# Linear tables by wide products, a shorter way to the mean of h, two more idle products and another written order

## The chip, the core and the metric

The kernel runs on one core of a Trainium2 chip. Its engines work side by side, each through its own queue in order: PE (TensorE) multiplies matrices and writes to PSUM, ACT (ScalarE) and DVE (VectorE) read PSUM and SBUF, POOL (GpSimd) reads and writes SBUF and starts some of the transfers, SP (SyncE) starts the others. The metric is the device time of one execution in microseconds (us), the median of the runs shown.

## The reference

Two attention steps over four batches of 12416 rows with 128 channels, and then a feed-forward network on every row:

```python
def mab(q, kv):
    s = scale * (q @ kv.transpose(0, 2, 1))
    s = s - s.max(-1, keepdims=True)
    a = np.exp(s)
    a /= a.sum(-1, keepdims=True) + 1e-09
    return a @ kv
h = mab(I, x)          # 32 inducing rows, per batch
attn = mab(x, h)       # every row of x is a mean of the 32 rows of h
gate = np.maximum(attn @ w_gate, 0.0)          # 128 -> 1536
out = (gate * (attn @ w_val)) @ w_out          # 1536 -> 128
```

`x` is (4, 12416, 128), `inducing` (32, 128), the weights have 1536 hidden channels, and the output is (49664, 128) in float32.

## The kernel before

**What it computes instead.** A row of the attention output is a weighted mean of 32 vectors. Where a hidden channel's gate has one sign for all 32 of them, the network's output for a row is a quadratic form in the row's 32 weights. The kernel builds this form once per batch as tables, and checks at the end that the signs were as assumed (if not, a general kernel runs; it doesn't here). With p the 32 exponentials of a row, the output is a sum over squared differences (p_m - p_n)^2 times tables `T`, plus a sum over p_m^2 times a linear table `L`, divided by the square of the sum of p.

**Stages of one batch b (1 to 3).** POOL starts the loads of x as float16 chunks of 16 row tiles (`x16`, line 237). Each chunk is transposed to `xT`, by PE with copies on DVE or ACT (lines 780 to 787) or by a transposing DMA on SP's queue (line 769). PE multiplies with the inducing rows (line 796), ACT takes exponentials (801), PE sums (810, 815), DVE adds up in `hz`. `h_join` and `h_centre` divide and centre h, giving `hT`. Gate and value products follow (line 898), DVE and ACT bring them to SBUF as `ga` and `va`, products of the two (lines 950, 957, 988, 1002) are multiplied by `w_out` on PE into the tables (lines 963 and 1007). Batch 0 is done first, by `first_batch`, from loads through SP.

**The output stage.** Each chunk of 2048 rows (`Q`, 24 of them and one for the rest) goes through: scores (PE, line 511), exponentials `p` (ACT, 520), p squared (POOL or DVE, 530), differences (PE, 567: four groups of 32 rows side by side, two of them into the tile `dd`, two into other banks), squares of `dd` (ACT, 581), squares of the other two banks (ACT at 593, or DVE copies at 595 and POOL or DVE multiplies at 599), 64 output products with T (PE, 625) and 16 with L (614), the division by the squared sum (DVE, 655), and the store on SP (673, 676). The squared reciprocals come from lines 545 (DVE) and 550 (POOL or DVE).

**The order.** From the tables of batch 0 on, every step (1588 or so of them) stands in a text, `ORDER`, three or more letters a step: which step, which engine, which of the rotating buffers (six PSUM banks `mb`, twelve `F`, and so on), and whether PE does some idle products first. Engines execute their steps in the order of the text, each waiting for what it needs. A choice that a step leaves open (DVE or POOL, DVE or ACT; a PE sum of two tables by 24 products, "left apart", in place of an addition at line 1002 and 12 products; transposing by PE or DMA) is made in the text too. A second rule holds in `in_turn`: a POOL step of some kinds (products of `ga` and `va`, their sums, squares, zq) waits for the last DVE step of these kinds that stands before it.

**The places that the change touches.** `centre` takes h (32 columns in float32) and writes `hT`: h times 64 minus its mean, then h times 64 twice, then the mean. Before, DVE sums h (line 246), scales the sum (247) and then subtracts (250), scales twice (259) and copies (267). At the end of `first_batch`, `idle` has PE do three products that nobody reads (line 358), while DVE computes h. `lin(b, 2)` adds the two halves `lt` of the linear table's operand, 384 elements a partition, and `lin_mm` multiplies it by `w_out` (line 963): for each of 12 groups of hidden channels four products with the same 32 columns, into the four groups of 32 PSUM partitions, so that the table stands there four times over. It is needed four times since p squared lies in four groups of 32 partitions.

Of the kernel before, what the change touches and what calls it, by code (L numbers as in the profile page):

```python
# [9 lines left out]
FP32 = mybir.dt.float32  # L10
# [93 lines left out]
Lo0M60Oz00Le000050Ov04P103LU0N94Mp4LK4P302MG0O+2P02O-2011Ow2Oy2Ox2P21H609E0GE006001002e052P41022007  # L104
10u0310I9042B0812f10J1PD2PB2PE2PC20CC015A0A10K10G10E10D10v10M1PP0PQ00PJ0PK048M0PL0PM0PN01M0PR0PS0PG
2PI2PH2P62P520O00519PT0Pb0Pc030x020P10S10Q1PO2P720y2PF2Pd0Pe0Me00+00428Pf07U0LY0611020z3PV30w32LW05
M+00U003041210-1Pg2LZ2PU2042LX1Li072Lj21G003171H11I2FM0Lg001m040P805Lh2P921K1PA11A002361C21B11n11E1
Ls080Lt2PW01PX0Lq05NV01131D2Pa214002051511811620d04Ck00b010Z0Lr20f00a0MT00W01y003241c050Y01b01d01+2
0531731o311J30c201z1201MA090MB2M8030e0Ni00g01s001234s02E01P00LL40Ly4M921e03+01i0La0030h21w21f251t11
u11h00o041g028002120q0Lb10m050p01j02912C21k20X022003110k00r01S000l00j01Q02A12312612411-22g20LQ0121T  # L110
0MI010s240n2MJ2LR11O042q0053ALz430i41l40t43641p011q22u12s12r11R0LS02EU0Lc01MR3MS30LT21U231Y0Lk013A6
04O051Ll12w00209Ld2Ph21r22D22y22+24P12x11V0Lm01Lu0031X01W04Q22Md31Lv14U0052B3W0004V14Y13X1Ln21Z24W2
2z31x2Mo322J012L0Lw032k004502K02I0Lx22m22o22l1M2012MC0032Q00M312G02-32p24X3Mz33MD130004573112N0M402
2M213422P02O0MK013321ML13c00158M522R24R02ME04MM033d13g13e14S2MF2MN2Mg010MO22a02Mi04Mh2MP032H05Mj1MQ
23o00106N8343532n34T3NJ352Z02V02b02Y02W02h043q13s13p12U02T02c222i22X22j23Y31NU3Ps01Pm03Pq00Pt1Pr13u
00245Pn2Pp2Po2H+0Pi053G013N003Z033H03I03M0Pj2Pl2Pk23v13w13y13a23B053F03O03i0032137043j13k13m13A03L0
3T03S03D03Q03R0P-2P+2Pv33J203P25Pu24m001323b3Pw34J003C03U24o14q14n13E21a42S4NK45k4Mq423V4A+4O244E02
4G0N20544D04I04F04L04K0N316c04a00134410Q12Q02Q624e14c1Px0570042QC27114b1Pz14203Q701Q804H24Q23QD04QE
0QB2Py25G020QH24g001534M25H1MX0444h1MY24504404702NL47NA40OD42d44004k15S000474904304A07305480Q325U15
W146235I305T152005104z04680314i16917424B24u05e00520Q52QI25g14w0NX014-05J035004x0Dc04y053215f1NY24+2  # L120
5i1Q435705550580Mk0005605Y0012AMl15K24v0459255444N4MV03QJ00QK05C05D05B0MW26A21QO25Z15c15a15M00539QN
15Q15N15A0MZ012QP01QQ0Jk0N0005O25E25P3Ng372326E00358QT2Ma1N12Mm046201Mb026F16G26I1Nh31Mc26K00036640
6B055-026505z06006306L16O1Mn25L26M2QU26C26W004055l0356a16Y25r05v05+06X1Mv0006N36H366226125o05q0Mw16
74OZ44C46Q004116R18m0207u0015w05p06U26S27v18n15s215t0N40115u07C004035x27x03Nm062N516V36T37G15y45F4I
s4Nt4OO43K4Mx01Nk056r006t07D17E17y2Nn2Ns306Z38o30753My26D37I00322NF001N604Nl2N727K27L3O1327z36u06s0
NQ0157J1NG17M16f047O00134NR16v247P17S26y0NH026w06e050NI27Q1760032B7T2OC337w317717827A26m06x0NZ0016z
06n06l0Na19e0326+2792ON348A0012A9f16o0NS048B16p22Nb036g06h06i06j0NT2Nc2Nd28E18C17+00040Ne036k27m027
r017l07k0Ke07j0Ok0OY357B3Oj3Nf28017-18217X084005097n238518627p0Qd037o07q0Qe17s2Qf04QV028738G0053788
1Qg1QW2QY2QX2QZ018I18H18K1Qa2Qc2Qb27a007b07Z07g047Y07W08s00258Qn2Qo28u18w18t1Qi39g328e017f07e07d08c
08b08d0AW0317h217c28P02AX192005468f259418p008R038T08i08Y018W09316q46-4O343Nu48OE498O08q29619q000519  # L130
s1Qv2Qp2Qq28X08g08V09h048h0AZ008Q09r1Qh39i2Aa29u18Z208y004058S0Qw05Om018j0Q-2901Qx0R0008U28k28z1On1
Q+1R10Qj38r39800314Qt29C2R428+1Qk059918l4D8020D91Qm19A19a049Y0Qs29b0A000102Bs09H029W09Z0A21A11A41Qr
2Ql29D39c229U09K03No0119T09V0Np1Qu29I0Ao00543OP44Aq1R52Ap19J09N009O09L09P09Q09X2RB39G0As19w0015B9M2
49R29x1Oa45Nq02R604R70Nr29+29y1Ai00309Aj1O8002Nz0119-39j3DA31RA2Ak2Am2RC05N+1O91RD09k004307i49l1AH0
0AG0N-019o2RG2BO0229m1Ac0035AAn2O029p3AY30Al3BP1Ag2Ad1AD01OJ014BR02AI0AB0A80OK1BS2Ae2Bm00527Bn1Bo2A
F0AC0AA0OA03AJ25Bq1BU00458OB2AE2BV1Ah3Af3BT3Ab3Bp3OL009S48a49d47t4BY2OU003AT02Oo011AQ0OM2BW2OV1Op1A
u00505A903Ay2Aw2Av1CG041BZ3Ax3BX3Az3BQ32DB01AR0Oq00AS0AO0CH1DC2Of015CM00146Og1CO2CN1AL0AM0AN0OW05AU
21Oh01CQ1OX2AP2Oi2Or2Bg00254Bk1B204B50B40BG03BD0B30Bi2Bh1Os2A-010Ba00522B624Bb1BE0B70BF0BI0B90Bc2Bj
3DD3Bd3CI30BH20Be1CY00450B80BA0CZ1Ca2BB2BJ0BL0BK0Cc1CS00231C004By01CJ05BM2AV4AK4BC4BN4E0002CT1Bu0CW
2CK2CU2E11Ce0035BB-0Cf1Cg2E300Ot02C10Bw0Bx0E42Ou2Ci1DQ0030ADS1DR1Bz0C805C20C70C60C50CB03B+22C32Bv0D  # L140
U1CL3CV3E53CX3Cb3Ch3CP3E232DE00219C923RM04DI1DF1RI00RS05RN2RP2RQ01CD0CC0CA0RO2RT2RR1DG1RJ2RL2DK0045
5RK2CE2DL1RH2Rg2DO1DM1Cq01Cp0Co0Eu021Cr0E600033E71Cu05Cv0Cm0Ct0Cw0EA2RU3Cs21EB3DW00432Cx2Ev1E81DY1C
+01Fm020D00Cz0C-0D200DX1Rd2Rc2Cn0Fn1F400547D40D30D50Dg02Dh0Di0D125Ew30F51F82F61Da1Ra2Fy00144De05Dj0
Fz1D62RV3Dk24Do0Dl0Dn0Dm0EO00308Rb2F+1G01EP1Dp2Dy02Dx0Dz0Dt01Ds0Dw0Df0Ri2EQ1ES1EI00456Du0Dr0D+20Re3
EJ1Ro0Rp03Rj00Rk0Dv2D-4D74CF4C44Cy4EC00210Rq0EK1EM1EG2Rn2ED1Ex04Rr0Ge052Rs0Ey2Rf2EE1Gf1E+00101Rt2F0
2EH3E-1EY04Ed02Ef0Ea0Eg0EW0Rh2F21Gk0053BEe0Gl1RW3Eh20Eb0EZ0Ej01El0Ek0Ec2FA0002AGo1Gm1Ru2Em0FB1Eo03E
p0Er0Eq0FC2EX0FE1R+2Fs00455Rv00Ft1Rw0En25RX02Rz2Es2FG00102F93Gg31Ez3Fo32Fw1Fu1R-05RZ1FI2RY2S00FH1IO
031S32FO041FK2IP1G200259FJ2G31FQ0Fp00FR0FS0Fq2G42FX0FT0G61Ia00303FL3FU23Ib1Ic2FV0FY0FW0Fg02G53F13FD
3FP05Ie1FZ2G800430G91GC2GA2Fi0Fc0Fh0HW000HX1Gq00138GB2Fb0Gs2Gr1Fe0GI04GL0Fd0Gu1Fr2GD3Ff22Gw00016Gy2
Gx1HY30Id3Gz3Gt3GJ0GO03Fj0GK0Fk2GG0G+1Hu00507GM21Hw2Et4Fa4Ei4Hv1GQ0GN0GP0GT02GU0GW0GR2Hy1Hc00141Hd1  # L150
He2IR05Ga00Gb0Gh03GV0GH0IS2Gi2Hg1H00015AGX25H11H22HB03GZ0GY0HC0H804Gc2H41Gj3Hf3H33Ho00212Hp1Hq2Hs2I
Q32Ht3IT3Hx3HA0HH0HG0HD0L4002L51IU00520HE23IV1IY2HF0HS01HR0HI0H900IW1HJ2Hi00329Hj1Hm2HN0HZ05HL0HQ0H
a2HT0KA040Hk1HU20Im00254KB1Iq2Hb3Hr3Hn3In1HM0IE03IL01HO0IK0I10Io1HP2SA2KM00455HK4GS4KO2KN1II0IG0IJ0
ID0IF0KQ1KY00026KZ1I204I40I705I30Ir3KP3KC31IZ3I00IM23IH2Kc2Ka1Ig0013BIh1Ii2I90I50L702I80IA0L82I621J
G001Ik1KG00128IB2JH1J504Iw03Ix0J60KI2KK2Ij3KH1J80J105J70HV4IN4Dq4Fl4IC4KS0001AIt02KW1S42S72J920KJ3L
93JI30Kd3KT1J00I-0JB0J20JD0Iy0Iz0J323KU1Je00141I+2Jf1JA0Kk05JC0Kq00Ko0Ji2Kg0JE2Jg1JM00342Kl0KD02JN1
JO2KE2Kj0Kr0Ku01Ki0KF3JQ1JP3KL3JS00329Km24Kp0Kx0Kv0Kw0JT1Ks2JW2Kh04J44Gd4Kt4JF4JU1JY00507Jc1L10K+0J
J03L00J+02JZ1S92Ky22Kn4Kz4K600K-0JK2SB2JL2JX2Jn0Ja1L22LA00133Jj3L632K50K40K70J-0K10K00K821K22LC1LD1
LB1Jw05Ju0Jx0Jv0S52Jm01L34K94Jr0Jy23K34Jz4S604SC2S82Jp0Jo0Jq0LE03LF0Js2LG0LH0SD2Jt4LI25SE00SF2LJ4SG
4"""  # L160
# [7 lines left out]
def square_body(ctx, tc, x, inducing, moe_w_gate, moe_w_val, moe_w_out, out):  # L168
    nc = tc.nc
# [74 lines left out]
    def centre(b, h):  # L244
        hb = st([P, 2], FP32, "hb", 2)
        nc.vector.tensor_reduce(out=hb[:, 0:1], in_=h, axis=AX.X, op=ALU.add)
        nc.vector.tensor_scalar(
            out=hb[:, 1:2], in0=hb[:, 0:1], scalar1=HS / M, scalar2=1.0, op0=ALU.mult, op1=ALU.mult
        )
        nc.vector.tensor_scalar(  # L250
            out=hT[b][:, 0:M],
            in0=h,
            scalar1=HS,
            scalar2=hb[:, 1:2],
            op0=ALU.mult,
            op1=ALU.subtract,
        )
# [9 lines left out]
        nc.vector.tensor_copy(out=hT[b][:, 2 * M + H :], in_=hb[:, 1:2])

    def first_batch(sp, psum):
# [185 lines left out]
        nc.vector.tensor_tensor(out=h, in0=hT_ps, in1=rzs[:, 0, :], op=ALU.mult)  # L455
# [950 lines left out]
```

## Time and profile before

| | us |
|---|---|
| median of 3 runs | 240.86 (239.56 to 243.02) |
| the profiled execution | 241.52 |
| its span, from first to last instruction | 239.8 |
| PE, DVE, ACT, POOL busy | 223.0, 202.5, 203.2, 132.4 |

The profile is of one execution. A line of a group names the line of the kernel, the engine, the operation, the tiles written and read, shapes, the count, the busy time with the mean duration of one in ns, and the idle time of the engine just before with what ended it. PEld is PE's weight load, which runs beside its products; two products that follow each other overlap, so the mean duration of one is longer than the distance between two. In a timeline a line has the start, the time that the group took, the engine and the operation.

### The profile page before, as it was taken

The page shows a single profiled execution, that of the slowest core. Times are in us where ns is not written, and L with a number is a line of the kernel's source. Part 1 is how long each engine was busy: PE and PEld are TensorE (multiplying, and loading weights), DVE is VectorE, ACT ScalarE, POOL GpSimd, SP SyncE. Part 2 cuts the span into 40 slices and gives each one's busy share as a digit, 9 for nine tenths or more (in the row PEclk, how much of TensorE's full clock was granted, in tenths as well). Part 3 has the DMA queues.
Part 4 walks back from the last instruction along what each step waited for, and adds up shares of the span by engine and source line. Part 5 has one row for each costly group of instructions (what it writes and reads, how often), then busy time and mean ns, then how long its engine had stood idle before and what let it go on. Part 6 is the DMA issues. An engine that isn't in the chain of part 4 may idle for free.

```text
span 239.8 us, 9824 instructions
## 1 busy us (share of the span) xinstructions
PE 223.0 (93%) x4209; PEld 174.5 (73%) x4209; DVE 202.5 (84%) x437; ACT 203.2 (85%) x366; POOL 132.4 (55%) x165
## 2 busy tenths in 40 slices
PE   5869899899989799999999999999999999999991
PEld 1668367788878578877887877876687677777880
DVE  3655799797979788887999988799998998989892
ACT  3665699789988699899999999798999999998940
POOL 4544807701745325678433289968336479895520
PEclk9999799999999999999999999999999999999998
DMA  6997899997999995389999999260007442077683
GB/s 227 414 394 297 104 214 212 157 210 208 228 225 213 171 215 227 60 294 200 249 277 190 200 254 398 92 247 31 4 0 307 166 161 79 27 297 293 264 302 104
DMA packets 36080, 49.22 MB, mean 205 GB/s; under 512 B 24224, under 2 KB 24896, under 8 KB 36032
## 3 DMA queue, kind: packets, MB, share of 16 engines
q1 hardware_dynamic: 31408, 38.61, 52.3%
q0 software_dynamic: 4576, 9.93, 23.4%
q8 instruction: 33, 0.54, 0.9%
q14 instruction: 15, 0.12, 0.2%
q10 hardware_dynamic: 48, 0.02, 0.1%
HBM read 27.80 MB, written 25.43 MB: 222 GB/s over the span
## 4 chain that ended last, share of the span: by engine, by line
PE 65%; DMA 24%; ACT 3%; DVE 3%; issue 2%; POOL 1%; SPq 0%; DVEq 0%; ACTq 0%
PE mb L625 32%; DMA x16q<-in_x_dram 8%; PE dd L567 6%; DMA x<-in_x_dram 6%; DMA x16r<-in_x_dram 6%; PE mb L567 5%; PE mb L614 4%; PE mb L1007 4%; DMA w<-in_moe_w_val_dram 4%; PE mb L810 3%; PE mb L796 3%; PE mb L511 2%; PE mb L780 2%; DVE osb L655 2%; ACT F L581 1%
## 5 line engine op out<-in xcount | busy, mean ns | idle before, releaser
L581 ACT ACTIVATE F<-dd 128x1024 f16<-128x1024 f32 x97 | 100.6, 1037 | 6.4 <-PE mb L567 2.8
L625 PE MATMUL mb<-T,F 128*128 128x128 f16 x1536 | 105.7, 219 | 0.1
L625 PEld LDWEIGHTS <-F 128*128 128x128 f16 x1536 | 87.1, 98 | 16.7 <-issue 14.8
L599 POOL TENSOR_TENSOR F<-F 128x512 f16<-128x512 f16 x61 | 62.7, 1041 | 31.7 <-DVE F L595 8.6
L593 ACT ACTIVATE F<-mb 128x512 f16<-128x512 f32 x122 | 71.1, 612 | 3.5 <-PE mb L567 1.9
L655 DVE TENSOR_TENSOR osb<-mb,zr 128x512 f32<-128x512 f32 x97 | 64.7, 682 | 5.7 <-PE mb L625 1.7
L595 DVE CAST F<-mb 128x512 f16<-128x512 f32 x72 | 48.2, 680 | 5.4 <-PE mb L567 3.5
L567 PE MATMUL mb<-p,diff 32*128 32x512 f16 (+1 forms) x200 | 39.7, 377 | 0.3 <-DVE osb L655 0.3
L567 PE MATMUL dd<-p,diff 32*128 32x512 f16 (+1 forms) x200 | 38.1, 377 | 0.4
L530 POOL TENSOR_TENSOR pp<-p 128x512 f16<-128x512 f16 (+1 forms) x21 | 21.2, 1012 | 7.0 <-DVE U L988 5.0
L567 PEld LDWEIGHTS <-diff 32*128 32x128 f16 x400 | 14.4, 91 | 9.5 <-issue 3.2
L520 ACT ACTIVATE p<-mb 128x512 f16<-128x512 f32 (+1 forms) x25 | 14.8, 598 | 4.2 <-PE mb L511 3.5
L614 PE MATMUL mb<-L,pp 32*128 32x128 f16 x384 | 17.3, 216 | 0.0
L1007 PE MATMUL mb<-wo,U 128*128 128x128 f16 x240 | 16.4, 219 | 0.1
L988 DVE TENSOR_TENSOR U<-va,ga 128x1536 f16<-128x1536 f16 x16 | 15.9, 1010 | 0.0
L1007 PEld LDWEIGHTS <-U 128*128 128x128 f16 x240 | 13.8, 98 | 1.8 <-issue 1.4
L614 PEld LDWEIGHTS <-pp 32*128 32x128 f16 x384 | 10.7, 93 | 5.1 <-issue 1.1
L389 DVE COPY xT<-xT_ps 128x1024 f16<-128x1024 f16 (+1 forms) x15 | 8.7, 582 | 6.4 <-PE xT_ps L385 6.2
L375 POOL CAST x16f<-x 128x512 f16<-128x512 f32 (+2 forms) x14 | 7.9, 567 | 10.7 <-DMA x<-in_x_dram 10.7
L375 ACT CAST x16f<-x 128x512 f16<-128x512 f32 (+2 forms) x15 | 7.7, 517 | 7.0 <-DMA x<-in_x_dram 7.0
L988 POOL TENSOR_TENSOR U<-ga,va 128x1536 f16<-128x1536 f16 x3 | 8.8, 2924 | 8.6 <-DVE U L1002 8.6
L237 POOL DMA_DIRECT2D x16q<-in_x_dram x18 | 10.2, 572 | 5.4 <-PE mb L815 5.4
(157 smaller groups left out, 308.9 us busy)
## 6 DMA issues: line engine op xcount, KB each, us to landing
out_dram<-osb SPq DMA_DIRECT2D x44, 512.0 KB, 4.1
x16q<-in_x_dram POOLq DMA_DIRECT2D x18, 512.0 KB, 9.7
x<-in_x_dram SPq DMA_DIRECT2D x9, 512.0 KB, 6.6
out_dram<-osb SPq DMA_DIRECT2D x9, 256.0 KB, 2.2
x<-in_x_dram SPq DMA_DIRECT2D x6, 256.0 KB, 9.2
w<-in_moe_w_gate_dram SPq DMA_DIRECT2D x1, 768.0 KB, 8.3
w<-in_moe_w_val_dram SPq DMA_DIRECT2D x1, 768.0 KB, 8.9
wo<-in_moe_w_out_dram POOLq DMA_DIRECT2D x1, 384.0 KB, 5.9
```

The source lines that it names most:

```text
L375: f(out=dst[:, a:b, :], in_=x32[:, a:b, :])
L530: engines[e].tensor_tensor(out=p2b[slot["pp", Q]][:, 0:w], in0=a, in1=a, op=ALU.mult)
L567: nc.tensor.matmul(bs[r][:, o], diff[rows, 4 * jj : 4 * jj + 4, :].rearrange("p k m -> p (k m)"), pb[slot["p", Q]][rows, 0:w], start=True, ...
L581: act.activation(out=Fb[slot["F", Q, j]][:, pair(j), :], in_=dd, func=AF.Square, accum_out=None if k is None else spread(Q, k),)
L593: act.activation(out=dst, in_=src, func=AF.Square, **more)
L595: dve.tensor_copy(out=dst, in_=src)
L599: engines[e].tensor_tensor(out=a, in0=a, in1=a, op=ALU.mult)
L614: nc.tensor.matmul(mb[slot["m", "o", Q, r]][:, t * P : (t + 1) * P], p2b[slot["pp", Q]][rows, t * P : (t + 1) * P], L[(Q // NQ) % 2][rows, :],
L625: nc.tensor.matmul(ps[:, t * P : (t + 1) * P], Fb[slot["F", Q, j]][:, r, t * P : (t + 1) * P], T[Q // NQ][:, j, :], start=start, stop=stop,)
L655: dve.tensor_tensor(out=o[:, 4 * (r % 2) : 4 * (r % 2) + 4, :], in0=mb[slot["m", "o", Q, r]].rearrange("p (t c) -> p t c", t=4), in1=rz.un ...
L988: engines[e].tensor_tensor(out=U[i][:, :, 4 * j : 4 * j + 4, :], in0=a[:, :, 0:M].unsqueeze(2).broadcast_to([P, NFF, 4, M]), in1=bass.AP(c ...
L1007: nc.tensor.matmul(ps, U[i][:, t, 4 * j : 4 * j + 4, :].rearrange("p k m -> p (k m)"), wo[:, t, :], start=(i, t) == (0, 0), stop=(i, t) == ...
```

## The change

The sum of h comes from the instruction that makes h (an accumulating output), now scaled so that the result is the mean; the separate sum and its scaling are gone, and h itself is scaled by 32 in place of 64, as it was multiplied by 2 already. The addition of the two halves of the linear operand writes it four times over (1536 elements a partition, into a new tile `lt4`), and PE does 12 products with 128 columns in place of 48 with 32. The idle products at the end of the first batch are 5 in place of 3. The order text is another throughout. In it, beside places in the queues, engines differ: 74 DVE copies at line 595 (72 before) and 120 ACT squares at 593 (122), 15 multiplies at 599 on DVE (11) and 59 on POOL (61), all four of the last linear additions on DVE (one on DVE, three on POOL), two of the other linear products on DVE (three) and six on POOL (five), 30 products at 988 on DVE (29) and two on POOL (three), six tables left apart (four), seven additions at 1002 on DVE (ten) and three on POOL (two), six table outputs on ACT (two) and ten on DVE (14), two PSUM-to-SBUF copies of transposes on ACT (four) and 16 on DVE (15), with the same 16 of them of full width in all, two copies of values on DVE (one), one of the linear tables' copies at 497 on ACT (none), 23 of the small squares at 550 on POOL (20), 11 chunks transposed by DMA (10, the added one is the single tile that is left over in batch 3), and two more idle products of the order's own (7 in place of 5).

```diff
 ORDER = """
...
-    def centre(b, h):
-        hb = st([P, 2], FP32, "hb", 2)
-        nc.vector.tensor_reduce(out=hb[:, 0:1], in_=h, axis=AX.X, op=ALU.add)
+    def centre(b, sums):
+
+        h, mean = st([P, M], FP32, "h", 2), st([P, 1], FP32, "hb", 2)
+        nc.vector.scalar_tensor_tensor(
+            out=h, in0=sums, scalar=HS / M, in1=rzs[:, b, :], op0=ALU.mult, op1=ALU.mult, accum_out=mean
+        )
         nc.vector.tensor_scalar(
-            out=hb[:, 1:2], in0=hb[:, 0:1], scalar1=HS / M, scalar2=1.0, op0=ALU.mult, op1=ALU.mult
-        )
...
+            out=hT[b][:, 0:M], in0=h, scalar1=float(M), scalar2=mean, op0=ALU.mult, op1=ALU.subtract
         )
...
-        idle(idle_ps, 3, xT[0][:, 0:4, :].rearrange("p t c -> p (t c)"))
+        idle(idle_ps, 5, xT[0][:, 0:4, :].rearrange("p t c -> p (t c)"))
 
         nc.vector.reciprocal(out=rzs[:, 0, :], in_=z1)
-        h = first["h"] = st([P, M], FP32, "h", 2)
-        nc.vector.tensor_tensor(out=h, in0=hT_ps, in1=rzs[:, 0, :], op=ALU.mult)
-        centre(0, h)
+        centre(0, hT_ps)
...
+    lt4 = mt([P, NFF, 4, M], FP16, "lt4")
...
         else:
-            eng.tensor_tensor(out=lt[0], in0=lt[0], in1=lt[1], op=ALU.add)
+            a, c = (l.unsqueeze(2).broadcast_to([P, NFF, 4, M]) for l in lt)
+            eng.tensor_tensor(out=lt4, in0=a, in1=c, op=ALU.add)
...
         for t in range(NFF):
-            for r in range(4):
-                nc.tensor.matmul(
-                    ps[32 * r : 32 * r + 32, :],
-                    lt[0][:, t, :],
-                    wo[:, t, :],
-                    start=t == 0,
-                    stop=t == NFF - 1,
-                )
+            nc.tensor.matmul(
+                ps,
+                lt4[:, t, :, :].rearrange("p k m -> p (k m)"),
+                wo[:, t, :],
+                start=t == 0,
+                stop=t == NFF - 1,
+            )
...
-            add(("lin", b, i), ("DVE", "POOL"), on + va_ + last(("Lm",)), [], f(lin, i))
-        add(("lin", b, 2), ("DVE", "POOL"), [("lin", b, 0), ("lin", b, 1)], [], f(lin, 2))
+            add(("lin", b, i), ("DVE", "POOL"), on + va_ + last(("lin", 2)), [], f(lin, i))
+        add(("lin", b, 2), ("DVE", "POOL"), [("lin", b, 0), ("lin", b, 1)] + last(("Lm",)), [], f(lin, 2))
```

More of the change, by code (lines that the diff above doesn't have):

```diff
@@ L163, in square_kernel @@
+v0JZ1K405Ko0JJ01K70Kr0Kp0Ky2JK2K50JX3L631JL3L93Ks2LA00215Jc1Ja1Kz4Kt4L34SB2S42LB1LC1LD1K60K103J-0Jl
+004J+0K00K823Ju0Jw0Jx0Jv0LE02K22S52Jy20SC2S605Jo0Jq0Jp0Jr0K34Jz4K94S82LF0LG0Js2LH0SD2Jt4LI21SE01SF2
+LJ4SG4"""
 def square_kernel(tc, x, inducing, moe_w_gate, moe_w_val, moe_w_out, out):
@@ L848, in h_centre @@
         dve.reciprocal(out=rzs[:, b, :], in_=mb[slot["m", "h", b]][:, 0:M])
-        h = st([P, M], FP32, "h", 2)
-        dve.tensor_tensor(out=h, in0=hz[:, 0:M], in1=rzs[:, b, :], op=ALU.mult)
-        centre(b, h)
+        centre(b, hz[:, 0:M])
     for b in range(1, B):
```

122 lines of the change are left out of this document (56 added, 66 removed).

## The prediction

> **What bounds the kernel now.** I read the page first for the busy engines and the chain that ended last, then the stages, then the one place where the clock of PE is low.
>
> ```profile
> span 239.8 us, 9824 instructions
> PE 223.0 (93%) x4209; PEld 174.5 (73%) x4209; DVE 202.5 (84%) x437; ACT 203.2 (85%) x366; POOL 132.4 (55%) x165
> PE 65%; DMA 24%; ACT 3%; DVE 3%; issue 2%; POOL 1%; SPq 0%; DVEq 0%; ACTq 0%
> ...
> core 0: us, PE busy (x) PEld busy (x) DVE busy (x) ACT busy (x) POOL busy (x), PEclk, DMA share, GB/s
> 0.00:25.00 25.00, 19.57 (x344) 14.62 (x344) 13.76 (x38) 13.56 (x33) 12.12 (x26) 1.00 0.83 319
> 25.00:48.00 23.00, 20.79 (x332) 14.87 (x332) 20.24 (x44) 20.02 (x35) 12.68 (x17) 0.93 1.10 180
> 48.00:230.00 182.00, 178.36 (x3482) 141.65 (x3479) 163.44 (x338) 168.81 (x298) 106.97 (x122) 1.00 0.73 195
> 230.00:239.80 9.80, 4.23 (x60) 3.37 (x57) 5.10 (x20) 0.78 (x2) 0.61 (x2) 0.89 0.48 166
> ```
>
> The reader is to see four stages. The first 25 us wait for the loads of batch 0. Then come 23 us in which the first tables are made and the output stage starts, 182 us of steady work, and a tail of 10 us. In the steady stage PE is busy 98% of the time, ACT 93% (168.81 of 182), DVE 90%: three engines near their limit, in order queues, so that no one edit moves the end by its own whole cost. The chain gives PE 65% and a DMA 24%; the DMAs in it are mostly the loads ahead of 48 us, which this change doesn't touch. The profiled execution took 241.52 us, 1.7 more than its span, and lies 0.7 above the median of 240.86.
>
> **The end of the first batch.** This is the only place with a stall that the change aims at by itself:
>
> ```profile
> 24.21 0.81 PE L358 MATMUL z1a_ps<-xT,eye 128*128 128x512 f16 x3
> 24.77 0.19 DVE L455 TENSOR_TENSOR h<-hT_ps,rzs 128x32 f32<-128x32 f32 x1
> 25.00 0.19 DVE L246 TENSOR_REDUCE hb<-h 128x1 f32<-128x32 f32 x1
> 25.22 0.15 DVE L247 TENSOR_SCALAR hb<-hb 128x1 f32<-128x1 f32 x1
> 25.41 0.24 DVE L250 TENSOR_SCALAR hT<-h,hb 128x32 f16<-128x32 f32 x1
> 25.72 0.15 DVE L267 CAST hT<-hb 128x1 f16<-128x1 f32 x1
> 26.02 0.57 PE L898 MATMUL mb<-hT,wg 128*128 128x81 f16 x6 [0.99 <-DVE hT L267]
> 26.51 0.62 PE L511 MATMUL mb<-xT,hT 128*32 128x512 f16 x4
> ...
> 57.33 0.40 PE L511 MATMUL mb<-xT,hT 128*32 128x512 f16 x4
> 27.31 0.60 ACT L520 ACTIVATE p<-mb 128x512 f16<-128x512 f32 x1 [1.35 <-PE mb L511]
> ...
> 25.00:26.00 1.00, 0.02 (x1) 0.01 (x1) 0.80 (x6) 0.96 (x1) 1.00 (x3) 0.97 0.00 0
> 26.00:29.00 3.00, 2.98 (x36) 1.70 (x40) 2.20 (x8) 1.57 (x4) 3.00 (x7) 0.50 1.39 142
> ```
>
> PE ends its three idle products at 25.02 and waits until 26.02 for DVE's chain. From 26 to 29 its granted clock is 0.50, so the first gates and scores take half as long again or more (four scores 0.62 us, and 0.40 later).
>
> *DVE's chain.* From the start of h (24.77) to the subtraction (25.41) are 0.64 us. One instruction with an accumulating output takes the place of three. The trace has none of this form with an accumulating output on DVE; its row without one takes 0.19 and the step to the next 0.23. Bounds: 0.23 (the sum is free) and 0.45 (it costs as much as the reduction after it). I take 0.25, so hT is there 0.4 us sooner (0.2 to 0.4).
>
> *The idle products.* Three take 0.81 us with the end of the last, so two more at most 0.54: PE is then busy until 25.5 instead of 25.02, while hT comes at about 25.47 plus the 0.15 to the first gate. They stand ahead of the gates in PE's queue; the cover is DVE's chain, and without it they would cost their 0.5 us. PE's gap shrinks from 1.0 us to about 0.1.
>
> *The clock.* If the gap is what lowers it, PE runs the next 3 us at 1.00. ACT's first exponentials wait for one group of gates and four scores; each loses about 0.2 us (0.62 less 0.40), and the differences after them as much: 0.6 us on the path to ACT's first squares, after which DVE and ACT are the slower ones until 40 us. I take 0.6, bounds 0 and 1.5 (half of the 3 us). Together the head gives 1.0 us, from 0.2 to 1.9.
>
> On that the Trainium skill, "TensorE: Matmul & The Clock Gate", Part 1, has a rule that speaks against it: the clock falls after an idle window of about 3.4 us that runs freely and doesn't start with the kernel. Here the low stretch is about that long, but the idle time before it is 1.0 us, and the pause of 1.6 us shown below, in the steady stage, has no low clock behind it (1.00 over the whole stage); by that rule the gap alone decides nothing, and the head would give 0.4. That is the fourth case below.
>
> **The tables and the instruction stream.**
>
> ```profile
> 189.11 0.79 PE mb L963 x48
> ...
> 93.52 0.67 PE mb L1007 x12
> ...
> q8 instruction: 33, 0.54, 0.9%
> PE mb L963 <- issue: 1.6, 1, 1.6
> PE mb L780 <- issue: 0.7, 1, 0.7
> ...
> 67.36:80.46 13.10, 12.40 (x256) 1.00 1.20 210
> ```
>
> Each linear table costs 0.79 us on the chain for 48 narrow products, as four of them run side by side; 12 wide ones (those of the other tables, line 1007) take 0.67. So the rewrite itself is worth 0.1 us a table, 0.4 in all (0 to 0.5), not a factor of four. But the last lines show more. PE stood still twice with nothing to wait for but its instructions, 0.7 us at 67.36 and 1.6 at 80.46, the latter inside a linear table (line 963). Between the two lie exactly 256 products with their 256 weight loads; 4209 products in 33 transfers of the instruction queue are 128 a transfer, so both pauses stand at an edge of such transfers, two apart. The change takes 144 products off, adds 24 for two more tables left apart and 4 idle ones, and one transpose less: 4092, one transfer fewer, and no place any more where 96 instructions pass in 0.8 us. Bounds: 2.3 us gained (both pauses gone), 1.6 lost (another one). I take half of the longer pause, 0.8.
>
> By the Trainium skill, "Runtime: NRT & Kernel Launch", section Instruction fetch mechanics, instructions come in blocks of 256 whose fetch is hidden. The 256 products between the two pauses agree with the block, while the 1.6 us speak against hidden; by that rule nothing would be gained here.
>
> **The rest by engines.** The order moves work between engines. From these rows:
>
> ```profile
> L957 DVE TENSOR_TENSOR lt<-lt,lt 128x384 f16<-128x384 f16 x1 | 0.3, 345 | 0.0
> L950 DVE TENSOR_TENSOR lt<-va,ga 128x384 f16<-128x384 f16 x2 | 1.1, 547 | 0.0
> L988 DVE TENSOR_TENSOR U<-ga,va 128x1536 f16<-128x1536 f16 x13 | 12.5, 969 | 0.1
> L1002 DVE TENSOR_TENSOR U<-U,U 128x1536 f16<-128x1536 f16 x10 | 9.3, 942 | 0.0
> L595 DVE CAST F<-mb 128x512 f16<-128x512 f32 x72 | 48.2, 680 | 5.4 <-PE mb L567 3.5
> L599 DVE TENSOR_TENSOR F<-F 128x512 f16<-128x512 f16 x11 | 4.9, 450 | 0.1
> L1021 DVE TENSOR_SCALAR T<-mb,half 128x128 f16<-128x128 f32 x14 | 4.8, 342 | 1.6 <-PE mb L1007 1.6
> L787 DVE COPY xT<-mb 128x1024 f16<-128x1024 f16 x13 | 8.8, 680 | 1.8 <-PE mb L780 1.6
> L593 ACT ACTIVATE F<-mb 128x512 f16<-128x512 f32 x122 | 71.1, 612 | 3.5 <-PE mb L567 1.9
> L785 ACT COPY xT<-mb 128x1024 f16<-128x1024 f16 x3 | 3.2, 1069 | 1.0 <-PE mb L780 1.0
> L1019 ACT ACTIVATE T<-mb,half 128x128 f16<-128x128 f32 x2 | 0.7, 374 | 0.2 <-PE mb L1007 0.2
> ```
>
> The wide addition has 1536 elements, each operand repeated over a middle dimension, as at line 988: 0.97 us. Bounds are 0.94 (line 1002, nothing repeated) and 2.19 (four times the 0.547 of line 950, repeated innermost); the row with the same repetition is the nearest. Four of them are 3.9 us, where DVE had 0.35. DVE so gets +3.5 there, -0.5 (a product at 950 less), +1.4 (two casts at 595), +1.8 (four multiplies), +1.0 (a product at 988), -2.8 (three additions at 1002), -1.4 (four table outputs), +1.4 (two copies at 787), -1.4 for the shorter centring (0.35 in each of four batches: 0.19, 0.19 and 0.15 of work less some 0.2) and about -0.5 of small ones: +2.5 us. ACT gets -1.2 (two squares), +1.5 (four outputs at 374), -2.1 (two copies): -1.9. PE gets 24 products by 0.056 (0.67 over 12), +1.3, less the 0.4 of the linear tables: +0.9; its four idle products fall where it waits anyway. POOL loses about 3 us and has 45% idle.
>
> What that makes of the end: DVE has 18.6 us idle in the steady stage, which cover its 2.5 (if the work lands where DVE is full, they cost up to 2.5); ACT's 1.9 free time for others only where ACT was last. PE's 0.9 counts by its share of the chain, 65%: 0.6 us.
>
> **Sum.** 241.52 - 1.0 (head) - 0.8 (pause) + 0.6 (PE) = 240.3 for an execution like the profiled one; the same 1.2 us off the median give **239.7 us**. That the new order fits the chip better or worse than the old one has no row of its own: I take zero, and bound it by the rivals.
>
> **Rivals.** 2% of the median, 4.8 us, is about what a measurement of this kernel can tell from no change.
>
> ```profile
> ACT F L581 <- PE mb L567: 2.8, 4, 2.2
> POOL zr L550 <- DVE U L988: 8.5, 1, 8.5
> L1002 POOL TENSOR_TENSOR U<-U,U 128x1536 f16<-128x1536 f16 x2 | 6.2, 3102 | 1.8 <-DVE U L1002 1.8
> ```
>
> *The order closes the gaps, and it is faster.* ACT, at 93%, waited 2.8 us for differences, 2.2 of it at once. If that goes, and both pauses (1.5 more than in the sum), the time is 239.7 - 2.8 - 1.5 = 235.4. For it: these are single long waits, which another order can avoid. Against: no engine has less to do but ACT, by 1%.
>
> *The division waits behind a long sum on POOL, and it is slower.* In the new order 23 of 25 small squares (line 550) are on POOL, and three sums of 3.10 us; the square of Q=17 stands two places behind the last such sum and 13 steps ahead of its division, where 29 steps lay between. POOL's own queue, and the rule that it waits for DVE, once held such a square for 8.5 us. While the division waits, PSUM banks stay taken, PE stops, and ACT and DVE after it. One hold costs up to 3.1 us; from the second on it decides: 239.7 + 6.2 = 245.9. Against: before, POOL had two sums of this kind and PE lost nothing that shows there.
>
> *The clock falls all the same*, so that the idle products do not do what they say: 239.7 + 0.6 = 240.3.
>
> **Chances.** The forecast 0.48, with a range of its own from 237 to 242.5 (the head from 0.2 to 1.9, the pauses from -2.3 to +1.6); the better order 0.27; the held division 0.15; the low clock 0.10. So faster by over 2% has 0.27, within 2% 0.58, slower 0.15. The range reaches to the faster case and some way towards the slower one: 234.3 to 244.8.
>
> **What would show it.** In the changed profile, an accumulating instruction at 25 us and the first gates at about 25.6 with a granted clock of 1.00 up to 30 us; 12 products in about 0.67 us for each linear table; DVE near 205 us, ACT near 201; 32 transfers on the instruction queue, and PE's waits for issue without one of over 1 us. The prediction is wrong if the clock is low again, if the wide additions take 2 us, or if the waits of line 655 for POOL grow by some us.

## The result and the profile after

The changed kernel took 239.83 us (median of 17 executions, 238.90 to 241.12), the kernel before 242.37 (17 beside them, 239.56 to 243.96). The ratio is 0.9926 with a 95% interval of 0.9902 to 0.9951: 0.7% faster, within the 2% that counts as no change. The ratio leaves out the slower executions, of which the kernel before has some and the changed one none, so it lies nearer to 1 than the quotient of the medians. Measured twice more beside the kernels below, the changed kernel had medians of 239.57 and 239.85 and the kernel before 241.97 and 242.54; the ratios were 0.9894 (0.9839 to 0.9948) and 0.9983 (0.9951 to 1.0016). So the gain lies between 0.4 and 2.6 us by the three ratios, and the medians differ by 2.4 to 2.7 in all three. The profiled execution took 240.26, against 241.52 before.

The page of the changed kernel, its totals, instruction queue and chain:

```profile
span 238.4 us, 9612 instructions
PE 222.7 (93%) x4092; PEld 174.3 (73%) x4092; DVE 205.4 (86%) x433; ACT 201.7 (85%) x366; POOL 128.7 (54%) x164
...
q8 instruction: 33, 0.54, 0.9%
...
PE 66%; DMA 16%; DVE 11%; ACT 3%; issue 2%; POOL 0%; SPq 0%; DVEq 0%; ACTq 0%
```

DVE has 2.9 us more and ACT 1.5 less. A DMA has 16% of the chain in place of 24%, DVE 11% in place of 3%. The stages (columns as before):

```profile
25.00:26.00 1.00, 0.83 (x9) 0.33 (x7) 0.50 (x6) 1.00 (x1) 1.00 (x3) 1.00 0.00 0
26.00:29.00 3.00, 2.80 (x39) 1.32 (x38) 2.48 (x7) 2.43 (x6) 3.00 (x6) 1.00 1.33 135
25.00:48.00 23.00, 20.67 (x310) 14.59 (x308) 20.01 (x39) 20.05 (x37) 11.41 (x18) 1.00 1.09 188
48.00:230.00 182.00, 179.87 (x3413) 142.66 (x3407) 167.56 (x344) 168.16 (x298) 105.78 (x121) 1.00 0.71 196
...
60.00:90.00 30.00, 29.99 (x578) 24.65 (x575) 26.89 (x59) 27.71 (x53) 14.03 (x16) 1.00 0.95 213
```

PE's clock is 1.00 from 26 to 29 us, where it was 0.50. But from 25 to 48 us PE is busy for 20.67 us, as much as before (20.79, of which some 3 at the low clock). PE is busier between 60 and 90 us. The kernel before, same stretch:

```profile
60.00:90.00 30.00, 27.67 (x572) 22.56 (x569) 25.58 (x59) 25.86 (x48) 14.78 (x17) 1.00 1.09 211
```

29.99 less 27.67 are 2.3 us, which is the sum of the two waits for instructions (0.7 and 1.6) that the prediction quoted. That is busy time; how much of it reaches the end is read below, from marks that both kernels have. The head, in the timeline of the changed kernel and, last, its first squares of differences:

```profile
24.28 1.24 PE L353 MATMUL z1a_ps<-xT,eye 128*128 128x512 f16 x5
24.84 0.19 DVE L247 SCALAR_TENSOR_TENSOR h<-hT_ps,rzs 128x32 f32<-128x32 f32 x1
24.96 0.08 DVE L247 DVE_READ_ACCUMULATOR h<-hT_ps,rzs 128x1 f32 x1
25.08 0.27 DVE L250 TENSOR_SCALAR hT<-h,hb 128x32 f16<-128x32 f32 x1
25.39 0.15 DVE L262 CAST hT<-hb 128x1 f16<-128x1 f32 x1
25.69 0.39 PE L890 MATMUL mb<-hT,wg 128*128 128x81 f16 x6 [0.17 <-DVE hT L262]
...
28.15 1.05 ACT L575 ACTIVATE F<-dd 128x1024 f16<-128x1024 f32 x1
```

```profile
28.74 1.02 ACT L581 ACTIVATE F<-dd 128x1024 f16<-128x1024 f32 x1
```

The accumulating instruction takes 0.19 us and its readout is a second one of 0.08; from the start of h to the subtraction are 0.24 us, where they were 0.64. The first squares (the second fence is the kernel before) start 0.59 us sooner. Of the linear tables, the group of the wide additions, and then a table's products in the chain:

```profile
L950 DVE TENSOR_TENSOR lt<-lt,lt 128x1536 f16<-128x1536 f16 x4 | 3.8, 950 | 0.4 <-POOL lt L942 0.4
```

```profile
41.74 0.67 PE mb L955 x12
```

A wide addition takes 0.95 us, and a table's 12 products 0.67. From the list of waits of the changed kernel:

```profile
POOL zr L544 <- DVE U L980: 6.4, 1, 6.4
...
PE dd L561 <- ACT F L575: 1.3, 4, 0.5
...
PE mb L890 <- DVE hT L262: 1.1, 3, 0.7
...
PE mb L774 <- DMA x16q<-in_x_dram: 0.6, 1, 0.6
...
ACT p L514 <- POOL zr L544: 0.2, 1, 0.2
```

Of waits of PE's products for instructions ("issue") the list has none of 0.2 us or more any longer; in their place stand waits for squares, for hT and for batch 1's loads.

Where the lead comes from shows at a mark that each batch has once, the cast of the mean into hT at the end of the centring (its start, us):

| kernel | batch 0 | 1 | 2 | 3 | span |
|---|---|---|---|---|---|
| before | 25.72 | 70.13 | 117.68 | 164.01 | 239.8 |
| after | 25.39 | 68.54 | 115.54 | 161.91 | 238.4 |
| lead | 0.33 | 1.59 | 2.14 | 2.10 | 1.4 |

A third of a microsecond comes from the head. From there to the mark of batch 1, a stretch with the first pause, 1.26 are won; from there to the mark of batch 2, a stretch with the second and longer pause, only 0.55. Nothing is won after 118 us, and 0.7 is lost again between 162 us and the end. With another order in every stretch, this alone doesn't tell what each part of the change is worth.

### The profile page after: what moved, and what is told of

Same layout as the page of the kernel before. It is cut to its first block, busy times and chain, and to the rows that moved or that the text cites. A ratio compares the mean times of both kernels' runs of the same rounds, so it can differ in the third digit from the quotient of the medians.

```text
span 238.4 us, 9612 instructions
## 1 busy us (share of the span) xinstructions
PE 222.7 (93%) x4092; PEld 174.3 (73%) x4092; DVE 205.4 (86%) x433; ACT 201.7 (85%) x366; POOL 128.7 (54%) x164
## 4 chain that ended last, share of the span: by engine, by line
PE 66%; DMA 16%; DVE 11%; ACT 3%; issue 2%; POOL 0%; SPq 0%; DVEq 0%; ACTq 0%
PE mb L619 34%; PE dd L561 7%; DMA x<-in_x_dram 6%; DMA x16q<-in_x_dram 6%; PE mb L561 4%; PE mb L608 4%; DVE osb L649 4%; DMA w<-in_moe_w_val_dram 4%; PE mb L804 3%; PE mb L505 3%; PE mb L790 3%; PE mb L774 2%; PE mb L999 2%; ACT F L575 2%; DVE F L589 2%
## 5 line engine op out<-in xcount | busy, mean ns | idle before, releaser
L619 PE MATMUL mb<-T,F 128*128 128x128 f16 x1536 | 107.8, 219 | 0.1
L593 POOL TENSOR_TENSOR F<-F 128x512 f16<-128x512 f16 x59 | 60.6, 1042 | 31.8 <-DVE pp L524 8.8
L587 ACT ACTIVATE F<-mb 128x512 f16<-128x512 f32 x120 | 69.1, 607 | 2.9 <-PE mb L561 1.6
L589 DVE CAST F<-mb 128x512 f16<-128x512 f32 x74 | 49.6, 683 | 4.2 <-PE dd L561 2.6
L999 PE MATMUL mb<-wo,U 128*128 128x128 f16 x264 | 18.7, 219 | 0.0
L994 POOL TENSOR_TENSOR U<-U,U 128x1536 f16<-128x1536 f16 x3 | 9.3, 3099 | 16.7 <-DVE zr L544 7.8
L999 PEld LDWEIGHTS <-U 128*128 128x128 f16 x264 | 15.2, 97 | 1.8 <-issue 1.6
L608 PE MATMUL mb<-L,pp 32*128 32x128 f16 x384 | 16.2, 216 | 0.0
L980 DVE TENSOR_TENSOR U<-ga,va 128x1536 f16<-128x1536 f16 x15 | 14.4, 969 | 0.2
L980 DVE TENSOR_TENSOR U<-va,ga 128x1536 f16<-128x1536 f16 x15 | 14.5, 970 | 0.0
```

What stands on the lines that cost most here:

```text
L587: act.activation(out=dst, in_=src, func=AF.Square, **more)
L589: dve.tensor_copy(out=dst, in_=src)
L593: engines[e].tensor_tensor(out=a, in0=a, in1=a, op=ALU.mult)
L608: nc.tensor.matmul(mb[slot["m", "o", Q, r]][:, t * P : (t + 1) * P], p2b[slot["pp", Q]][rows, t * P : (t + 1) * P], L[(Q // NQ) % 2][rows, :],
L619: nc.tensor.matmul(ps[:, t * P : (t + 1) * P], Fb[slot["F", Q, j]][:, r, t * P : (t + 1) * P], T[Q // NQ][:, j, :], start=start, stop=stop,)
L980: engines[e].tensor_tensor(out=U[i][:, :, 4 * j : 4 * j + 4, :], in0=a[:, :, 0:M].unsqueeze(2).broadcast_to([P, NFF, 4, M]), in1=bass.AP(c ...
```

## The experiments

The question was which part gives the 1.8 us (0.7% of the time), and whether it does so by the way that the prediction gave.

### The head and the clock

Two kernels. In `head_alone` the kernel before gets the new centring and five idle products, and nothing else. In `new_idle3` the changed kernel gets three idle products again:

```diff
-        idle(idle_ps, 5, xT[0][:, 0:4, :].rearrange("p t c -> p (t c)"))
+        idle(idle_ps, 3, xT[0][:, 0:4, :].rearrange("p t c -> p (t c)"))
```

> The old order and the narrow linear tables, with the shorter way to the mean of h and five idle products. Theory 1: clock 1.00 from 25 to 30 us, first squares of dd 0.6 us sooner, and 0.6 to 1.0 us of it kept to the end: ratio about 0.996. Theory 2: the same at 28 us, and nothing left at the end, ratio 0.999 to 1.001.

> The changed kernel with three idle products at the end of the first batch in place of five. Theory 1: the gap of PE is 0.6 us, the clock falls from 26 to 29 us, and the time is 0.4 to 0.6 us over that of the changed kernel, ratio about 0.995. Theory 2: no difference to the changed kernel, ratio 0.993. If the idle time in front must be longer than 0.6 us for the clock to fall, the clock stays at 1.00 and the two cannot be told apart.

Measured: `head_alone` 242.13 us, beside 242.36 for the kernel before, ratio 1.003 (0.998 to 1.008): the head by itself gives nothing that shows. `new_idle3` 240.03, ratio 0.9964 (0.9924 to 1.0003), with no low clock behind a gap of 0.60 us, so its two theories can't be told apart. The kernel with the old code and the new order, `order_alone`, says more of the clock. It has three idle products, and its gates begin as late after them as before; the timeline, then the windows:

```profile
24.66 0.81 PE L358 MATMUL z1a_ps<-xT,eye 128*128 128x512 f16 x3
26.46 0.38 PE L898 MATMUL mb<-hT,wg 128*128 128x81 f16 x6 [0.99 <-DVE hT L267]
```

```profile
26.00:29.00 3.00, 2.54 (x42) 1.44 (x43) 2.03 (x11) 1.91 (x6) 3.00 (x7) 1.00 1.13 110
```

The same wait of 0.99 us, and a clock of 1.00. `wide_old` (below), which also has three idle products and the old centring, shows 1.00 there as well. So of the three profiles with a gap of 0.99 us (the third is that of the kernel before), one has the low clock and two have not; the other 11 have gaps of 0.17 to 0.64 us, and none has it there. The gap alone doesn't lower the clock, and whether a shorter gap keeps it up can't be told from so few. The low stretch of the kernel before lasted 3.41 us (25.94 to 29.35). The Trainium skill, "TensorE: Matmul & The Clock Gate", Part 1, has the clock judged by a window of about 3.4 us that runs freely; the length agrees, and such a window can also fall differently in executions of kernels that are alike up to there. It also says that the clock falls after an idle window, and there the trace differs, for PE was busy for 2.49 of the 3.41 us ahead of it (the kernel before):

```profile
22.53:25.94 3.41, 2.49 (x49) 1.65 (x46) 2.03 (x11) 2.29 (x4) 3.28 (x4) 1.00 0.05 18
```

And what became of the head's 0.3 to 0.6 us? PE's waits in `head_alone`:

```profile
PE mb L773 <- DMA x16q<-in_x_dram: 1.8, 1, 1.8
PE mb L773 <- issue: 0.8, 1, 0.8
PE mb L954 <- issue: 0.5, 1, 0.5
```

The first squares start at 28.28, 0.46 us sooner than before, but at 47 us PE stands 1.8 us for the loads of batch 1 (0.9 before), and goes on at 47.82 in place of 47.00. Those loads are started by POOL after other work, here even 0.25 us later than before (25.54 and 25.29), and a head that is quicker waits longer for them. What its profile is ahead by in the end, 0.3 us, comes from a second pause that is shorter in this execution (0.69 in the place of 1.85).

### The wide linear tables

`wide_old` is the kernel before with the wide addition (on DVE four times) and 12 wide products, its order otherwise untouched, and `new_narrow` the changed kernel with the 48 narrow products and the narrow addition:

```diff
-            a, c = (l.unsqueeze(2).broadcast_to([P, NFF, 4, M]) for l in lt)
-            eng.tensor_tensor(out=lt4, in0=a, in1=c, op=ALU.add)
+            eng.tensor_tensor(out=lt[0], in0=lt[0], in1=lt[1], op=ALU.add)
...
```

> The old order, old centring and three idle products, with the wide linear tables alone, all four additions on DVE. Theory of the work (wide products cost less by themselves): DVE +3.5 us, POOL -2.7, PE -0.4, so a ratio of 0.998 to 1.010. Theory of the block edges (PE pauses where its next block of 256 instructions is late, so fewer instructions move the edges): the 1.6 us pause inside the second linear table is gone, another may come elsewhere, ratio 0.990 to 1.003. Below 0.996 speaks for the edges, over 1.003 for the work.

> The changed kernel with the linear tables as before: 384 elements added, 48 narrow products each. Theory 1: DVE has 2.4 us less, PE 0.4 us more, 144 products and 144 weight loads come back: within 0.4 us of the changed kernel (ratio 0.991 to 0.995), unless a pause of over 1 us for instructions comes back inside a linear table, which then costs part of it. Theory 2 expects the same here; a third theory, that the wide products themselves bring the gain, expects a ratio of 0.997 or more.

Measured: `wide_old` 240.86 us, beside 241.97 for the kernel before (ratio 0.9988, 0.9961 to 1.0015) and 239.57 for the changed kernel. By the medians the tables give 1.1 us in the old order, by the ratio 0.3; the interval of the ratio includes no change, and the ratio lies between the two marks that the expectation set (0.996 and 1.003). `new_narrow` 242.03, ratio to before 1.005 (0.9995 to 1.0104), and 2.0 above `new_idle3` beside it (240.03; ratio of the two 1.008, 1.005 to 1.013), which has the wide tables. So in the new order the tables are worth about 2 us, and without them the change gains nothing that shows. In the old order their worth is not settled. Yet a linear table itself became only 0.12 us shorter (0.79 to 0.67).

Where the time goes shows when the profiled executions of a pair are laid beside each other. Both kernels of a pair follow the same order, and ACT squares `dd` 97 times in each. For the n-th time, this is the start in the first kernel and how much sooner (+) or later (-) it starts in the second; the values are worked out from the traces.

```
wide_old against before       new_narrow against after
  n   us, before  wide_old      n   us, after  new_narrow
 18      65.57     +0.29       10     49.27      -0.09
 19      70.41     +1.15       11     50.98      -0.34
 22      77.73     +1.09       16     60.92      -0.34
 23      83.25     +1.77       17     62.91      -0.77
 44     129.24     +1.76       19     68.31      -1.16
 46     134.68     +1.19       23     80.54      -0.64
 73     186.53     +1.17       36    108.95      -0.63
 74     188.29     +0.97       37    110.97      -1.40
 97     229.66     +0.98       74    186.50      -1.39
                               75    188.37      -1.52
                               97    227.03      -1.51
```

The differences come in steps. `wide_old` wins 0.9 us at 66 to 70 us, where the kernel before has its first pause, and 0.7 at 78 to 83, where that has its second and `wide_old` waits 0.9 itself, for DVE. It loses 0.6 around 131 us, where PE waits for the wide addition, and 0.2 near the last table. Its waits of PE:

```profile
PE mb L781 <- DVE osb L656: 0.9, 1, 0.9
...
PE mb L964 <- DVE lt L959: 0.3, 1, 0.3
```

`new_narrow` loses in steps at 50, 62, 67 and 110 us, and gets 0.3 back at 78. Of its four tables (42, 80, 132 and 187 us) only the last shows a loss, of 0.13. These are single executions, but both profiles of the old order with narrow tables (the kernel before and `head_alone`) have the two pauses, and both with wide ones (`wide_old` and `wide_old_head`) have none there. So the tables act on the time by when PE's instructions come, and in the old order some of it is lost again to waits for DVE.

### The pauses of the instruction stream

What `new_narrow` loses in its four steps, and what `wide_old` wins, are pauses of PE with no other cause in the trace. Here all of PE's instructions in the trace (products, weight loads, and the few waits and drains of its own queue) are numbered from 0 in their order of start, and a gap goes from one start to the next. Every gap of 0.55 us or more between 36 and 228 us for which the trace names no data stands in front of a number that leaves 193 when divided by 256. So do the smaller ones of `new_narrow`, 0.29 us at 50, 0.47 at 62 and 0.45 at 67 us. The rows are worked out from the traces; the last column goes from the end of the last transfer on the instruction queue to the instruction behind the pause:

```
kernel        next instruction   number  mod 256   gap us   transfer          from its end
before        L780 product       2241    193       0.91     65.67 to  66.59   1.46
before        L963 product       2753    193       1.85     79.47 to  80.66   1.43
head_alone    L773 product       2241    193       1.03     66.50 to  67.42   1.46
head_alone    L954 product       2753    193       0.69     78.63 to  80.59   1.22
order_alone   L625 product       4033    193       1.04    108.82 to 109.76   1.52
order_alone   L963 weight load   4801    193       0.99    131.31 to 132.26   1.39
new_narrow    L619 product       4033    193       0.83    107.71 to 109.24   1.47
new_idle3     L804 weight load   1985    193       0.84     60.71 to  61.70   1.46
after_again   L561 weight load   2497    193       0.59     72.55 to  73.51   1.45
early_wo      L619 weight load   2241    193       0.66     64.73 to  65.66   1.40
early_wo      L561 weight load   2497    193       0.62     71.67 to  72.63   1.45
```

So PE takes its instructions in blocks of 256, and at all 438 edges of the 14 profiles the first of a new block starts no sooner than 1.2 us after the block's transfer ends; behind a pause it is 1.2 to 1.5. The transfer takes 0.9 to 2.0. It begins as PE enters the block ahead of it, or up to 6.4 us later; for the two pauses of the kernel before it was 3.65 and 5.05 us later. PE pauses where it runs through a block in less time than these three together. Why some transfers begin late is not shown here. The Trainium skill, "Runtime: NRT & Kernel Launch", section Instruction fetch mechanics, gives the block of 256 and calls the crossing mostly hidden; the block agrees, but gaps of up to 1.85 us were not hidden here. The pause also differs between executions of one kernel: at number 2497 of the changed kernel the gap was 0.34, 0.59 and 0.34 in its three profiles.

If that is so, moving the edges against the work must change the time. `new_shift36` is the changed kernel with 36 more products in the first 6 us, where PE waits for the first loads, so that each later product stands 36 further on:

```diff
-        for _ in range(8):
+        for _ in range(5):
...
+        for _ in range(39):
+            nc.tensor.matmul(warm_ps[:, 0:1], eye16, warm[:, 0:1], start=True, stop=True)
```

> The changed kernel with 36 products more in the first 6 us, where PE waits for x (three of the eight warm products become 39 of one column), so that every edge of 256 instructions falls 36 products earlier in the work, as between 42 and 79 us of the kernel with narrow tables. Edge theory: pauses of 0.3 to 0.5 us near 50, 62 and 68 us as there, the lead at 70 us shrinks by 0.5 to 1.0, and the time is 0.3 to 1.0 us over the changed kernel. If edges don't matter, no difference beyond 0.2 us.

> The changed kernel itself, beside the others of this group, as their measure: ratio 0.990 to 0.996 by either theory.

Measured: 239.26 us, beside 239.57 for the changed kernel again, ratio of the two 0.999 (0.997 to 1.006): no difference, so the slowdown that was expected is a miss. In its profiled execution no edge has a gap of over 0.2 us, where the changed kernel has four of 0.2 to 0.35. But of the 1.0 us by which the span is shorter, 0.7 are there at 47 us already, as PE waited less for the loads of batch 1 (0.3 us; 0.6 in the changed kernel). That a pause at an edge costs time is shown by the steps above; that moving the edges changes the median isn't.

### The order by itself

> The code of before (three idle products, separate sum of h, 48 narrow products for each linear table) with the new order. Theory 1 (the head is worth about 1 us, the order little): the clock is low again from 26 to 29 us, ACT's first squares of dd start at about 28.7 us, and the time stands 0 to 0.8 us under before, ratio 0.997 to 1.000. Theory 2 (the new order makes the gain, what the head wins is waited away later): ratio as for the whole change, about 0.993.

> The old order with the wide tables, the new centring and five idle products: all of the change but the order. Theory A (the order by itself is worth nothing; the wide tables give 1.1 us through the pauses, and the head keeps 0.2 to 0.4): 239.6 to 240.6 us, within 0.6 of the changed kernel. Theory B (only the new order makes 2 us of the wide tables): 240.7 to 241.3, 0.9 or more above the changed kernel. In the trace by both: no pause of PE over 0.5 us between 60 and 85 us, first squares of dd at 28.2 to 28.4 us.

`order_alone` (old code, new order) took 242.45 us, beside 242.36 for the kernel before: equal by the medians, 1.9 us slower by the ratio (1.0078, 1.0032 to 1.0124). Two pauses are back in it, at other places (PE's waits):

```profile
PE mb L625 <- issue: 0.8, 1, 0.8
PE mb L963 <- issue: 0.8, 1, 0.8
```

`wide_old_head` is all of the change but its order: 240.65 us, beside 239.85 for the changed kernel (ratio of the two 1.003, 1.001 to 1.006). No pause is left between 60 and 85 us, as expected; the first squares came at 27.16, a microsecond too soon, since the loads of batch 0 were faster in that execution. The 0.8 us lie between what the two theories allowed (0.6 and 0.9), so how much of the order's worth hangs on the tables remains open. A second pair with narrow tables differs in the order alone, both with the new centring: `head_alone` with 242.13 us and `new_narrow`, beside it, with 242.03 (ratios to before 1.003 and 1.005). So with the wide tables the new order gains 0.2 to 1.5 us, and with the narrow ones no gain shows; whether it loses up to 2 us there, as the ratio of `order_alone` has it, is not settled.

### The loads of batch 1

If late loads swallow the head's gain, then earlier loads should bring it out. In `early_load` POOL starts batch 1's loads ahead of the load of `w_out`:

```diff
-        nc.gpsimd.dma_start(out=wo, in_=moe_w_out.rearrange("(i p) c -> p i c", p=P))
         nc.scalar.copy(out=wv, in_=w32[1])
         for q in range(NQ + 1):
             load_x(1, q, x16q[q] if q < NQ else x16r[1])
+        nc.gpsimd.dma_start(out=wo, in_=moe_w_out.rearrange("(i p) c -> p i c", p=P))
```

> The changed kernel with POOL starting the loads of batch 1 ahead of the load of w_out, 1.2 us sooner. If what the head wins is swallowed by the wait for these loads at 41 to 48 us, that wait (0.6 us in the changed kernel) shrinks and up to 0.6 us is kept to the end: ratio 0.002 under the changed kernel. If it is not, no difference; if w_out then comes late for the first tables, slower by up to 1 us.

It took 257.51 us, ratio 1.0643 (1.0583 to 1.0703), a clear miss, and one wait of PE says why:

```profile
PE mb L999 <- DMA wo<-in_moe_w_out_dram: 17.0, 1, 17.0
```

The load of `w_out` (384 KB) now stands in POOL's queue behind six loads of 512 KB, and the first table waits 17 us for it. The second attempt leaves that order and uses a gap instead. POOL waits 1.48 us for the gate weights; `early_wo` starts the load of `w_out` in that time, ahead of the cast:

```diff
-        nc.gpsimd.tensor_copy(out=wg, in_=w32[0])
         nc.gpsimd.dma_start(out=wo, in_=moe_w_out.rearrange("(i p) c -> p i c", p=P))
+        nc.gpsimd.tensor_copy(out=wg, in_=w32[0])
```

`early_wo_shift` adds the 36 products of `new_shift36`.

> The changed kernel once more, beside the other three. Both theories: 239.3 to 240.1 us.

> The changed kernel with POOL's start of the load of w_out (1.22 us) ahead of the cast of wg, in the 1.48 us in which POOL waits for the gate weights. The loads of batch 1 then start 1.1 us sooner, and everything else stays. Theory A (PE's wait for batch 1's first chunks between 41 and 48 us, 0.6 to 1.1 us, swallows what the head gains): that wait is gone and the time is 0.5 to 1.0 us below the changed kernel. Theory B (the wait costs nothing by itself, since ACT and DVE catch up behind it): the wait is gone and the time stays within 0.3 us.

> The same with 36 more products of PE in the first 6 us, so that every later product stands 36 further on against the edges of the blocks of 256. Theory A (an edge that falls where PE has slack saves time): 0.3 to 0.7 us below the kernel with the early load alone, no pause of PE at any edge over 0.3 us. Theory B (what the shifted kernel gained before was the missing wait for batch 1's loads in that execution): within 0.3 us of the kernel with the early load alone.

`early_wo` took 237.96 us, `early_wo_shift` 237.88, and the changed kernel beside them 239.85: ratios to it of 0.992 (0.991 to 0.995) and 0.992 (0.990 to 0.995); to the kernel before 0.987 (0.981 to 0.993) and 0.987 (0.981 to 0.994). Both are faster than these two, by 1.9 us and, by the ratio, about 3. POOL's timeline after the change and in `early_wo`, and the stage from 25 to 48 us of `early_wo`:

```profile
22.73 1.47 POOL L441 CAST wg<-w 128x1536 f16<-128x1536 f32 x1 [1.48 <-DMA w<-in_moe_w_gate_dram]
24.14 1.22 POOL L442 DMA_DIRECT2D wo<-in_moe_w_out_dram  x1
25.36 3.20 POOL L237 DMA_DIRECT2D x16q<-in_x_dram  x6
```

```profile
20.57 1.22 POOL L441 DMA_DIRECT2D wo<-in_moe_w_out_dram  x1
22.11 1.46 POOL L442 CAST wg<-w 128x1536 f16<-128x1536 f32 x1 [0.33 <-DMA w<-in_moe_w_gate_dram]
23.52 3.20 POOL L237 DMA_DIRECT2D x16q<-in_x_dram  x6
```

```profile
25.00:48.00 23.00, 22.20 (x351) 16.57 (x352) 20.94 (x36) 21.33 (x40) 9.52 (x15) 1.00 1.04 190
```

The cast starts 0.6 us sooner in this execution (its weights came sooner), the loads 1.8, of which 1.2 are the moved start. PE no longer waits for them at all, and is busy for 22.20 of the 23 us, where it was 20.67 after the change. Theory A of that run stands in its direction, with about twice the gain it allowed. The third profile of the changed kernel has room for that: there PE waited for those loads 1.8 us in two pieces, and against it the squares of `dd` in `early_wo` go from 0.35 us later at the first to 1.66 sooner at 46 us. Of these, 0.84 are lost again by 84 us, over two pauses, the last two of the table above. Of the shift, theory B stands: the two kernels are equal to 0.1 us. The profiled execution of `early_wo` is the longest of its six with 238.74; the other five lie between 237.89 and 238.07, and whether those five had no pauses can't be seen without a trace.

## Why the prediction was right, and where it wasn't

The forecast came true, no change at 2%, and the time was within 0.2 us: 239.7 predicted, 239.83 measured. So close a time is luck, for two errors met in it. The three executions of the kernel before had a median 1.5 us below that of the 17; and the gain was sized at 1.2 us where the ratio gives 1.8 (1.2 to 2.4) and the medians 2.5. Step by step:

- **DVE's chain, 0.4 us: right.** 0.64 became 0.24, and h cost 0.19 with a readout of 0.08, close to the value taken.
- **The clock, 0.6: wrong in its cause.** The clock was 1.00, and the first squares came 0.59 us sooner, but the gap alone didn't make it low: two kernels with the same gap ran at 1.00. Nor was the fourth case seen, "the clock falls all the same": in the three profiles of the changed kernel the clock is 1.00 there. What decides whether it falls stays open.
- **The head together, 1.0: mis-sized.** At hT 0.33 us were gained, and of that little stayed, since PE then waits for the loads of batch 1. The text said of these DMAs that the change doesn't touch them. It doesn't, but they were next in line: what was late next behind the head was not priced. `early_wo` is 1.9 us faster by an earlier start of them.
- **The pauses, 0.8: right in kind, mis-sized.** Both are gone, 2.3 us in the stretch from 60 to 90. The tables with their pauses give about 2 us there (`new_narrow`), where the sum had 0.4 for the tables beside the 0.8; in the old order 0.3 by the ratio and 1.1 by the medians. The reason given, fewer instructions, is not the whole one: each block of 256 still has an edge, and a pause stands where its transfer comes late.
- **The tables' own products: right.** 0.67 us each, 0.12 less.
- **PE's more work, +0.6, and the order, 0: not separable.** With the old code the order costs between nothing (medians) and 1.9 us (ratio), with the rest of the change it gains 0.8 (0.2 to 1.5). The sum's +0.6 lies between.
- **Loads of the engines: right.** DVE 205.4 (near 205 predicted), ACT 201.7 (near 201), the wide addition 0.95 (0.97). The instruction queue has 33 transfers as before, not the 32 that the products alone gave; why stays open.
- **The better order (235.4): half of its reason came true.** Both pauses went, but ACT's waits for differences did not: 7.9 us in all, with none over 0.8, where they were 4.9 with one of 2.2. In place of the single long wait stand many short ones. The squares of `dd` in the changed kernel, then the line that the prediction didn't show of the kernel before:

```profile
ACT F L575 <- PE dd L561: 4.0, 12, 0.8
ACT F L575 <- PE mb L561: 3.9, 10, 0.7
```

```profile
ACT F L581 <- PE dd L567: 2.1, 8, 0.5
```

- **The held division (245.9): not seen.** POOL's square was held for 6.4 us once, as the rival had it, but nobody waited for it longer than 0.2 us (ACT for `zr`, in the fence of waits above).

## What to carry to other kernels

When the head of a kernel is made shorter, look first at what lands next: here a load's start, moved into a gap of 1.48 us on its own queue, was worth as much as all of the change, while the head's own gain didn't show in the time. A wait for "issue" on a busy PE can be an edge of its instruction stream; count the instructions to the next such wait. When two kernels follow the same order, lay their executions beside each other at a mark that repeats: steps in the difference show where the time goes, which the sums of busy time don't. An order may have its worth with one version of the code alone, so undo code and order apart before naming a cause.

## What the runs showed of the hardware beside that

The centring has small DVE instructions of 0.15 to 0.3 us. In batches 2 and 3 single ones of them took 1 us. DVE and, below it, POOL in the changed kernel:

```profile
114.17 1.01 DVE L247 SCALAR_TENSOR_TENSOR h<-hz,rzs 128x32 f32<-128x32 f32 x1
...
160.04 0.94 DVE L250 TENSOR_SCALAR hT<-h,hb 128x32 f16<-128x32 f32 x1
160.90 1.09 DVE L254 TENSOR_SCALAR hT<-h 128x32 f16<-128x32 f32 x2
```

```profile
113.09 2.04 POOL L593 TENSOR_TENSOR F<-F 128x512 f16<-128x512 f16 x2 [0.90 <-DVE zs L829]
...
159.91 2.06 POOL L593 TENSOR_TENSOR F<-F 128x512 f16<-128x512 f16 x2
```

Each long one ends within 0.05 us of the end of a POOL multiply that was running when it began: 115.18 against 115.13, 160.98 against about 160.94 (the first of two), 161.99 against 161.97. In batch 0 POOL was starting transfers, and the same lines took 0.19 and 0.27. This agrees with the Trainium skill, "SBUF — State Buffer", section SBUF: two separate sides, by which GpSimd and some instructions of DVE share a pair of ports that one of them holds for a whole instruction. It bears on the change: in batch 3 DVE's shorter chain waits for POOL, and PE's longest wait for hT (0.7 us) stands behind it. The kernel before has such long ones there too (0.69 us at line 250, 1.10 for the two of line 259). No kernel that moves POOL's multiply away from that place was run, so the cost of it stays open, as does why the loads of batch 0 at 16 us came up to 1.5 us apart in executions of kernels that are alike up to there.
